# Scores of the backward pass as rows in column strips: extending them to the alternating stretch and the second chain

## The chip, the cores and the metric

The kernel runs on one core of a Trainium2 chip. The time is device microseconds of one execution. A ratio is the mean time of one kernel's fast runs over that of the other's of the same rounds on the same chip, so it is not quite the ratio of the medians quoted beside it. Each ratio comes with its 95% interval.

## The reference, cut to what matters

The program computes one adaLN block in decode (batch 2, one token, 32 heads, a K and V cache of 8192 rows of 128 bf16 per head) and all its gradients. Per head, of which there are 64:

```
scores = K q / sqrt(128);  p = softmax(scores);  o = p V           # forward: reads K and V
x1 = x + ga * (o Wo);  SwiGLU block;  the way back to d_o           # the "chain": short, serial
dp = V d_o                                                          # reads V again
dV = p (outer) d_o;   dK = ds (outer) q,  ds = p * (dp - sum(p*dp)) # writes 2 x 2 MB per head
```

K is read once, V twice (less a few heads kept), dK and dV are written once: 422 MB read and 284 MB written in all. The change concerns `dp = V d_o`, in the code's words "V times dO".

## The kernel before: the parts that matter

The program is laid out by hand in slots (the code below is shortened); a pass over one head takes 8 slots. Passes "A" are forward (K, then V), passes "C" are backward. The first 32 A passes (batch 0) run alone; then the first chain; then, from 500 to 1060 us about, A passes of batch 1 and C passes of batch 0 alternate; then the second chain runs together with 9 C passes; then the rest of the C passes run with the weight gradients.

Every pass transposes its head's blocks on TensorE, eight to a tile `kt`. Scores can then be made in two ways.

```python
def c_s(n, g):
    if n in crow:                                   # as rows, in four strips of 32 columns
        return s_rows(("c", n), n, g, ...)
    for j in range(GRP):                            # as columns: one matmul of one column a block
        nc.tensor.matmul(DP[n][:, cc:cc+1], kt[:, j, :], DO_bf[:, b, h:h+1], ...)

def s_rows(key, i, g, bank):                        # every second group: 4 matmuls of 512 columns
    w = qz[i % NZ][:, NSL-1-a:NSL-1-a+NR]           # weights 128 x 32, one column non-zero
    for j in range(NST):
        nc.tensor.matmul(R_ps[key][NR*j:NR*(j+1), :], w, kt[:, o:o+SW, :], ...)

def rows_out(key): nc.scalar.copy(t, R_ps.pop(key)) # row bank to SBUF (group "srow")
def cols_out(ps, t): ...                            # 4 fp32 matmuls turn it back into columns
```

The outer products of dV and dK are made by VectorE, half a head at a time, and stored from there by a queue that GpSimd issues in order. dK products start 11 slots after the pass's first slot, and one slot later for a head that goes by rows. Below, "M products" are the matmuls of line 480, the A passes' products with V.

```python
halfp = tile_pool(bufs=21)     # 21 tiles of 128 x 8192 bytes: all of K, V, dK, dV pass through them
for q in range(NQ):                                                  # NQ = 4
    at(s + 2*q, PL_TT, lambda: c_dv(n, q))
    at(s + NG + LAG + 1 + (n in crow) + 2*q, PL_DK, lambda: c_dk(n, q))
```

A load waits until one of the 21 half tiles is free. A half tile of dV or dK becomes free after its store.

Of the kernel before, what the change touches and what calls it, by code (L numbers as in the profile page):

```python
# [9 lines left out]
F32 = mybir.dt.float32  # L10
# [7 lines left out]
def kernel(  # L18
# [26 lines left out]
    nc = tc.nc  # L45
    P = 128
# [11 lines left out]
    NHD = B * H  # L58
# [4 lines left out]
    NG = KK // GRP  # L63
# [8 lines left out]
    def hb(i):  # L72
        return i // H, i % H
# [15 lines left out]
    kps = ctx.enter_context(tc.tile_pool(name="kps", bufs=1, space=bass.MemoryType.PSUM))  # L89
# [12 lines left out]
    def mtps():  # L102
        return mps.tile([P, 512], F32, name="m_ps", tag="m_ps")
# [10 lines left out]
    QP = 4  # L114
    NST = 4
    NR = P // NST
# [8 lines left out]
    NSL = KK // (SW * NST)  # L125
# [1 line left out]
    ssel = cst.tile([P, NSL * NST], F32, name="ssel")  # L127
    nc.vector.tensor_copy(ssel[:].rearrange("p (x j) -> p x j", j=NST),
                          identb[:].rearrange("p (j x) -> p x j", j=NST)[:, 0:NSL, :])
    NZ = 3  # L130
    qz = [cst.tile([P, NR + NSL - 1], BF16, name=f"qz{k}") for k in range(NZ)]
    for z in qz:
        nc.vector.memset(z[:], 0.0)
# [4 lines left out]
    def col(name, nch=NC, dt=F32):  # L138
        return cols.tile([P, nch, B], dt, name=name, tag=name)
# [51 lines left out]
    def kb_(store, i, kk):  # L191
        return store[(i, kk // HK)][:, kk % HK, :]

    def vb_(key, kk):
        return V[(key, kk // HK)][:, kk % HK, :]
# [24 lines left out]
    qT_bf = col("qT_bf", H, BF16)  # L220
# [108 lines left out]
    now = [0]  # L329
# [9 lines left out]
    def pump():  # L339
        while loads and free["half"] - keep[0] >= 1:  # L340
            loads.pop(0)[2]()

    def release(n=1):
        free["half"] += n
# [3 lines left out]
    def head_ps():  # L348
        t = stps()
        cur_ps[:] = [t, now[0], 0]  # L350
        return t
# [22 lines left out]
    def transposes(block, dve):  # L374
        tp = tps.tile([P, GRP, P], BF16, name="tp", tag="tp")
        for j in range(GRP):
            nc.tensor.transpose(tp[:, j, :], block(j), identb[:])  # L377
        kt = ktp.tile([P, GRP, P], BF16, name="kt", tag="kt")
        if dve:
            nc.vector.tensor_copy(kt[:], tp[:])  # L380
        else:
            nc.scalar.copy(kt[:], tp[:])  # L382
        return kt
# [3 lines left out]
    def a_t(i, g):  # L387
        b, h = hb(i)
        if g == 0:
            if i in byrows:  # L390
                nc.gpsimd.tensor_copy(qz[i % NZ][:, NSL - 1:NSL], qT_bf[:, h, b:b + 1])
            else:
                S_ps[i] = head_ps()
        kts[(i, g)] = transposes(lambda j: kb_(K, i, g * GRP + j), g in (2, 6))
# [3 lines left out]
    def s_rows(key, i, g, bank):  # L398
        if g % SG < SG - 1:
            return  # L400
        def kt_of(k):
            return (*key, k) if isinstance(key, tuple) else (key, k)
        a = g // SG
        if a == 0:
            R_ps[key] = bank()
        w = qz[i % NZ][:, NSL - 1 - a:NSL - 1 - a + NR]
        for j in range(NST):
            kt = kts[kt_of(g - SG + 1 + j * SW // GRP)]
            o = j * SW % GRP
            nc.tensor.matmul(R_ps[key][NR * j:NR * (j + 1), :], w, kt[:, o:o + SW, :],  # L410
                             start=(a == 0), stop=(a == NSL - 1))
        for k in range(SG):
            kts.pop(kt_of(g - k))
# [18 lines left out]
    def a_s(i, g):  # L432
        if i in byrows:
            return s_rows(i, i, g, mtps)
        b, h = hb(i)
        kt = kts.pop((i, g))
        for j in range(GRP):
            cc = g * GRP + j
            nc.tensor.matmul(S_ps[i][:, cc:cc + 1], kt[:, j, :], qT_bf[:, h, b:b + 1], start=True, stop=True)  # L439
# [106 lines left out]
    def job_a(i, s):  # L546
        x = 1 if i in byrows else 0
        MOFF = moff(i)
        for g in range(NG):
            at(s + g, PL_T, lambda g=g: a_t(i, g))  # L550
            at(s + g + LAG, PL_S, lambda g=g: a_s(i, g))
            at(s + g + MOFF, PL_M, lambda g=g: a_m(i, g))
            at(s + g + MOFF, PL_FREE, lambda g=g: a_free(i, g))
        if x:
            at(s + NG + LAG, PL_EXP, lambda: a_rows(i))
            at(s + NG + LAG + 1, PL_EXP, lambda: a_cols(i))
        at(s + NG + LAG + x, PL_MAX, lambda: a_max(i))
        at(s + NG + LAG + x + 1, PL_MAX, lambda: a_bias(i))
        at(s + NG + LAG + x + 2, PL_EXP, lambda: a_exp(i))
        for q in range(NQ):  # L560
            at(s + NG + LAG + x + 3 + 2 * q, PL_TT, lambda q=q: a_scale(i, q))
        at(s + MOFF, PL_EXP, lambda: a_pz(i))
        at(s + MOFF + 2, PL_T, lambda: a_kp(i))
        at(s + MOFF + 2, PL_FREE, lambda: k_free(i, 0))
        at(s + MOFF + 4, PL_FREE, lambda: k_free(i, 1))
        if i % HPB == HPB - 1:
            at(s + MOFF + 3, PL_EXP, lambda: a_kp_rows(i))
            at(s + MOFF + 4, PL_M, lambda: a_kp_out(i))
        at(s + MOFF + NG - x, PL_EV, lambda: a_evac(i))
# [8 lines left out]
    def end_a(s):  # L578
        return s + MOFF + NG
# [68 lines left out]
    def hcol(name, dt=F32):  # L648
        return cols.tile([P, B, H], dt, name=name, tag=name)
# [7 lines left out]
    DO_bf = hcol("DO_bf", BF16)  # L657
# [384 lines left out]
    def lay(steps, slot):  # L1042
        for n, f in steps:
            at(slot, PL_TASK, f)
            slot += n
        return slot
# [15 lines left out]
    sC = []  # L1062
# [16 lines left out]
    R0 = min([sA[i] for i in byrows], default=sA[NHD - 1])  # L1079
    A_END = end_a(sA[NHD - 1]) + 1  # L1080
# [5 lines left out]
    t1 = lay(ch[1], CS1)  # L1086
# [42 lines left out]
    def c_t(n, g):  # L1129
        if g == 0:  # L1130
            if n in crow:
                b, h = hb(n)
                nc.gpsimd.tensor_copy(qz[n % NZ][:, NSL - 1:NSL], DO_bf[:, b, h:h + 1])
            else:
                DP[n] = head_ps()
        spare = A_END <= now[0] < t1 or now[0] >= max(sC) - 5 * NG
        kts[("c", n, g)] = transposes(lambda j: vb_(("c", n), g * GRP + j), g in (2, 6) and not spare)
        if g % HG == HG - 1:
            V.pop((("c", n), g // HG))
            release()  # L1140
            pump()

    crow = {n for n in range(NHD) if t1 < sC[n] < max(sC) - 4 * NG}

    def c_rows(n):
        kts[("crow", n)] = rows_out(("c", n))
# [4 lines left out]

    def c_s(n, g):
        if n in crow:
            return s_rows(("c", n), n, g, lambda: kps.tile([P, QP * P], F32, name="k_ps", tag="k_ps"))
        b, h = hb(n)
        kt = kts.pop(("c", n, g))
        for j in range(GRP):
            cc = g * GRP + j
            nc.tensor.matmul(DP[n][:, cc:cc + 1], kt[:, j, :], DO_bf[:, b, h:h + 1], start=True, stop=True)  # L1159
# [53 lines left out]
    for n in range(NHD):  # L1213
        s = sC[n]
        for g in range(NG):
            at(s + g, PL_T, lambda n=n, g=g: c_t(n, g))
            at(s + g + LAG, PL_S, lambda n=n, g=g: c_s(n, g))
        at(s - 3, PL_B, lambda n=n: c_spread(n))
        for q in range(NQ):
            at(s + 2 * q, PL_TT, lambda n=n, q=q: c_dv(n, q))  # L1220
            at(s + NG + LAG + 1 + (n in crow) + 2 * q, PL_DK, lambda n=n, q=q: c_dk(n, q))
        x = 1 if n in crow else 0
        if x:
            at(s + NG + LAG, PL_EXP, lambda n=n: c_rows(n))
            at(s + NG + LAG + 1, PL_EXP, lambda n=n: c_cols(n))
        at(s + NG + LAG + x, PL_DS, lambda n=n: c_ds(n))

        for hf in range(2):
            if n not in kept:
                want(s + hf * HG, lambda n=n, hf=hf: load_v(("c", n), n, hf))  # L1230
# [185 lines left out]
    for kc in range(NC):  # L1416
        for half in range(HD // 2048 if HD >= 2048 else 1):
            w = min(2048, HD)
# [27 lines left out]
    for kc in range(NC):  # L1446
        for m0 in range(0, MD, 2048):
            w = min(2048, MD - m0)
# [72 lines left out]
```

## Time and profile before

1744.36 us, median of 6 runs (1740.22 to 1746.57).

The table by stretches of the kernel before. Its columns are: the stretch, its length, busy time (and instructions) of TensorE, its weight loads, VectorE, ScalarE and GpSimd, then the granted TensorE clock, the mean busy share of the 16 DMA engines, and GB/s moved.

```profile
60.00:260.00 200.00, 199.93 (x4125) 185.08 (x4123) 128.41 (x178) 126.86 (x178) 73.69 (x118) 1.00 1.01 416
500.00:1060.00 560.00, 448.61 (x6855) 385.46 (x6853) 387.74 (x457) 296.88 (x444) 84.47 (x243) 0.86 1.01 420
1060.00:1120.00 60.00, 49.06 (x901) 45.88 (x899) 46.88 (x85) 33.07 (x52) 9.36 (x18) 0.75 0.91 358
1120.00:1200.00 80.00, 63.28 (x1317) 59.17 (x1316) 65.56 (x124) 74.32 (x95) 13.32 (x25) 0.93 1.01 412
1200.00:1240.00 40.00, 15.16 (x176) 11.56 (x175) 12.93 (x14) 11.44 (x18) 2.33 (x5) 0.59 1.01 426
1240.00:1600.00 360.00, 282.60 (x2283) 181.43 (x2282) 224.33 (x248) 224.37 (x345) 51.55 (x103) 0.62 1.01 414
```

Of these stretches DMA is saturated in all but 1060 to 1120 us, the start of the second chain. TensorE is called busy for 80% of the alternating stretch, but that is not what limits it. The waits of TensorE in that stretch (engine, line, what it waited for, us in total, times, longest):

```profile
PE tp L377 <- DMA half<-in_A_k_cache_dram: 65.5, 26, 5.7
PE s_ps L430 <- ACT srow L417: 23.1, 22, 1.1
```

and the waits of the queue that issues the loads:

```profile
SPq L187 <- DMA out_dram<-half: 338.9, 64, 11.5
SPq L181 <- DMA out_dram<-half: 102.1, 22, 5.4
```

So TensorE waits for loads of K, and loads wait for stores that free half tiles. The cost of the pieces comes from the timeline of TensorE in that stretch (start, us, engine, line, operation, count). Starts are what to read: durations of pipelined matmuls overlap.

```profile
634.03 0.40 PE L410 MATMUL m_ps<-kt,qz_108 128*32 128x512 bf16 x4
634.37 0.64 PE L480 MATMUL m_ps<-ek,half 128*128 128x129 bf16 x8
...
638.02 1.06 PE L430 MATMUL s_ps<-ssel,srow 128*128 128x16 f32 x8 [1.05 <-ACT srow L417]
638.93 0.94 PE L377 MATMUL tp<-identb,half 128*128 128x128 bf16 x8
639.66 0.40 PE L1159 MATMUL s_ps<-DO_bf,kt 128*128 128x1 bf16 x8
639.92 1.01 PE L377 MATMUL tp<-identb,half 128*128 128x128 bf16 x8
```

Four strip matmuls take 0.34 us from start to next start; eight one-column matmuls take 0.26 us, about 30 ns each; the way back into columns takes 0.91 us after a wait of 1.05 us. The Trainium skill ("TensorEngine Tiling (Array Packing)", section Instruction Overhead) says that a matmul of one column takes as long as one of 60 columns. The lines above agree in kind: eight transposes of 128 columns take 0.73 us (638.93 to 639.66), so 128 times the columns cost 2.8 times the time. A one-column matmul is wasteful by the column but cheap by the piece.

### The profile page before, as it was taken

Reading aid. Unit: us, or ns where it says so; the run is one execution under the profiler, and the core shown is the slowest. Engines: PE = TensorE matmul, PEld = TensorE weight load, DVE = VectorE, ACT = ScalarE, POOL = GpSimd, SP = SyncE. Lnnn points to the kernel's source line nnn. Section 1 sums busy time; section 2 is a strip of 40 time slices with the busy share of each in tenths; the row PEclk is TensorE's granted clock in tenths of the full one; section 3 lists DMA queues with packets and bytes.
Section 4 is the critical chain, followed back from the end, with each engine's and each line's share of the span. In section 5 each row is a group of like instructions: output and inputs, shape, how many; then the busy total and the mean of one; then the engine's idle time right before and its main releaser. Section 6 shows DMA issues by size and latency. Waiting matters only on the chain.

```text
span 1739.6 us, 50825 instructions
## 1 busy us (share of the span) xinstructions
PE 1418.5 (82%) x22083; PEld 1182.0 (68%) x22083; DVE 1154.6 (66%) x1574; ACT 1030.7 (59%) x1506; POOL 328.5 (19%) x696
## 2 busy tenths in 40 slices
PE   6999999989988788778787887885589797775684
PEld 5999998879877676667776666875355454454463
DVE  2666666867876667676676766785566667656676
ACT  4666666646565555455554555696467566665685
POOL 0334333322211111111111111111111111111111
PEclk9999999988988889888888888798655557668787
DMA  9999999999999999999999999999999999999998
GB/s 381 416 416 416 416 416 389 416 383 390 378 397 423 425 424 422 424 408 424 405 423 424 418 411 375 367 422 421 425 404 423 413 416 392 422 417 402 408 418 334
DMA packets 109388, 709.07 MB, mean 408 GB/s; under 512 B 11175, under 2 KB 17683, under 8 KB 27243
## 3 DMA queue, kind: packets, MB, share of 16 engines
q1 hardware_dynamic: 67280, 421.59, 59.7%
q0 software_dynamic: 36864, 268.45, 37.2%
q10 hardware_dynamic: 5019, 15.78, 2.3%
q8 instruction: 173, 2.83, 0.6%
q14 instruction: 52, 0.43, 0.1%
HBM read 421.57 MB, written 284.20 MB: 406 GB/s over the span
## 4 chain that ended last, share of the span: by engine, by line
DMA 33%; PE 33%; issue 21%; DVE 5%; ACT 4%; POOL 3%; SPq 1%; POOLq 0%; ACTq 0%; DVEq 0%
DMA half<-in_A_k_cache_dram 19%; PE tp L377 13%; DMA out_dram<-half 10%; PE m_ps L480 10%; PE s_ps L439 3%; PE k_ps L502 2%; ACT kt L382 2%; POOL out_dram L1187 2%; DVE half L1182 2%; DMA half<-in_A_v_cache_dram 2%; DMA half<-in_w_mod_dram 1%; DVE ek L465 1%; PE m_ps L410 1%; DMA half<-in_A_wo_dram 1%; PE s_ps L430 1%
## 5 line engine op out<-in xcount | busy, mean ns | idle before, releaser
L382 ACT COPY kt<-tp 128x1024 bf16<-128x1024 bf16 x794 | 798.1, 1021 | 600.8 <-PE tp L377 572.3
L377 PE MATMUL tp<-identb,half 128*128 128x128 bf16 x8192 | 734.7, 243 | 114.0 <-DMA half<-in_A_k_cache_dram 69.1
L377 PEld LDWEIGHTS <-half 128*128 128x128 bf16 x8192 | 582.7, 110 | 207.6 <-issue 127.8
L480 PE MATMUL m_ps<-ek,half 128*128 128x129 bf16 x4096 | 341.4, 228 | 4.7 <-DVE ek L465 2.9
L1187 POOL DMA_DIRECT2D out_dram<-half x256 | 136.7, 534 | 985.6 <-DVE half L1182 871.1
L380 DVE COPY kt<-tp 128x1024 bf16<-128x1024 bf16 x230 | 158.4, 689 | 246.3 <-PE tp L377 245.7
L480 PEld LDWEIGHTS <-half 128*128 128x128 bf16 x4096 | 261.5, 101 | 17.1 <-issue 16.7
L1159 PE MATMUL s_ps<-DO_bf,kt 128*128 128x1 bf16 x2496 | 112.7, 166 | 30.0 <-DVE kt L380 15.9
L1159 PEld LDWEIGHTS <-kt 128*128 128x128 bf16 x2496 | 104.6, 102 | 37.0 <-DVE kt L380 16.3
L430 PE MATMUL s_ps<-ssel,srow 128*128 128x16 f32 x400 | 65.0, 297 | 57.5 <-ACT srow L417 57.3
L439 PE MATMUL s_ps<-qT_bf,kt 128*128 128x1 bf16 x2496 | 107.7, 164 | 1.2 <-DVE lnst L1027 0.4
L430 PEld LDWEIGHTS s_ps<-ssel,srow 128*128 128x128 f32 x400 | 60.0, 230 | 67.3 <-ACT srow L417 67.0
L439 PEld LDWEIGHTS <-kt 128*128 128x128 bf16 x2496 | 96.7, 97 | 2.0 <-issue 1.0
L1315 ACT CAST stg<-m_ps 128x512 bf16<-128x512 f32 (+2 forms) x124 | 72.6, 588 | 16.2 <-PE m_ps L1314 7.7
L502 PE MATMUL k_ps<-half,pz 128*32 128x512 bf16 x1024 | 71.7, 402 | 4.6 <-POOL pz L488 4.6
L1314 PE MATMUL m_ps<-half 2*128 2x512 bf16 (+2 forms) x124 | 66.8, 538 | 5.4 <-ACT half L1289 2.8
L451 DVE TENSOR_REDUCE nm<-s_ps 128x1 f32<-128x128 f32 x64 | 18.7, 291 | 52.3 <-PE s_ps L448 52.3
L502 PEld LDWEIGHTS <-pz 128*32 128x32 bf16 x1024 | 22.7, 99 | 27.8 <-POOL pz L488 6.1
L1314 PEld LDWEIGHTS <-half 2*128 2x128 bf16 (+1 forms) x124 | 12.6, 101 | 32.8 <-issue 27.7
L1397 ACT COPY kt<-tp 128x1024 bf16<-128x1024 bf16 x28 | 30.5, 1089 | 4.1 <-PE tp L1391 3.0
L1289 ACT CAST half<-m_ps 2x512 bf16<-2x512 f32 (+1 forms) x36 | 20.2, 565 | 19.0 <-DMA out_dram<-half 14.9
L793 PE MATMUL s_ps<-d_attn_bf,kt 128*128 128x1 bf16 x256 | 11.4, 165 | 22.7 <-DVE kt L780 12.7
(899 smaller groups left out, 1912.5 us busy)
## 6 DMA issues: line engine op xcount, KB each, us to landing
out_dram<-half POOLq DMA_DIRECT2D x256, 1024.0 KB, 13.5
half<-in_A_v_cache_dram SPq DMA_DIRECT2D x252, 1024.0 KB, 16.8
half<-in_A_k_cache_dram SPq DMA_DIRECT2D x128, 1024.0 KB, 19.9
out_dram<-stg ACTq DMA_DIRECT2D x22, 512.0 KB, 9.9
half<-in_A_wq_dram SPq DMA_DIRECT2D x8, 1024.0 KB, 11.6
half<-in_A_wo_dram SPq DMA_DIRECT2D x4, 1024.0 KB, 20.6
half<-in_w_mod_dram SPq DMA_DIRECT2D x3, 1024.0 KB, 16.7
half<-in_B_w_dram SPq DMA_DIRECT2D x3, 1024.0 KB
```

Of the source, the lines that this page charges most:

```text
L377: nc.tensor.transpose(tp[:, j, :], block(j), identb[:])
L380: nc.vector.tensor_copy(kt[:], tp[:])
L382: nc.scalar.copy(kt[:], tp[:])
L430: nc.tensor.matmul(sv[:, c, :], t[:, c * P:(c + 1) * P], ssel[:], start=True, stop=True)
L439: nc.tensor.matmul(S_ps[i][:, cc:cc + 1], kt[:, j, :], qT_bf[:, h, b:b + 1], start=True, stop=True)
L480: nc.tensor.matmul(m[:, 0:P + 1], vb_(i, kk), t[:, kk % QK, 0:P + 1], start=(kk == 0), stop=(kk == KK - 1), skip_group_check=True)
L502: nc.tensor.matmul(kp["ps"][NR * j:NR * (j + 1), :], pz[:, o:o + NR], K[(i, kk // HK)][:, kk % HK:kk % HK + QP, :], start=False, stop=(h = ...
L1159: nc.tensor.matmul(DP[n][:, cc:cc + 1], kt[:, j, :], DO_bf[:, b, h:h + 1], start=True, stop=True)
L1182: nc.vector.tensor_tensor(pair(t[:, o:o + QK, :]), QD[(n, which)][:].rearrange("p (a b) -> p a b", b=2).unsqueeze(1).to_broadcast((P, QK, ...
L1187: sq_.dma_start(src_of(dst, n)[:, hf * HK:(hf + 1) * HK, :], t[:])
L1314: nc.tensor.matmul(ps[:lw, 0:rw], rsl(ln, lc, lw, step), rsl(rn, rc, rw), start=True, stop=True)
L1315: nc.scalar.copy(st["t"][:lw, o:o + rw], ps[:lw, 0:rw])
```

## The change

The intent is to take one-column matmuls from TensorE where passes alternate and in the second chain: 34 more heads take V times dO as rows (before, only 25 late heads did). A fourth weight tile is added so that A and C passes have two each, and the strip rows go to the bank `m_ps` while the bank `k_ps` is in use.

```diff
-    NZ = 3
+    NZ = 4
     qz = [cst.tile([P, NR + NSL - 1], BF16, name=f"qz{k}") for k in range(NZ)]
...
-                nc.gpsimd.tensor_copy(qz[i % NZ][:, NSL - 1:NSL], qT_bf[:, h, b:b + 1])
+                nc.gpsimd.tensor_copy(qz[i % 2][:, NSL - 1:NSL], qT_bf[:, h, b:b + 1])
...
-        w = qz[i % NZ][:, NSL - 1 - a:NSL - 1 - a + NR]
+        w = qz[i % 2 + (2 if isinstance(key, tuple) else 0)][:, NSL - 1 - a:NSL - 1 - a + NR]
...
-                nc.gpsimd.tensor_copy(qz[n % NZ][:, NSL - 1:NSL], DO_bf[:, b, h:h + 1])
+                nc.gpsimd.tensor_copy(qz[2 + n % 2][:, NSL - 1:NSL], DO_bf[:, b, h:h + 1])
...
-    crow = {n for n in range(NHD) if t1 < sC[n] < max(sC) - 4 * NG}
+    crow = {n for n in range(NHD) if R0 < sC[n] < max(sC) - 4 * NG}
+
+    def c_bank():
+        if now[0] <= A_END:
+            return mtps()
+        return kps.tile([P, QP * P], F32, name="k_ps", tag="k_ps")
...
-            return s_rows(("c", n), n, g, lambda: kps.tile([P, QP * P], F32, name="k_ps", tag="k_ps"))
+            return s_rows(("c", n), n, g, c_bank)
```

`R0` is the first slot of the alternating stretch, `A_END` the end of the last A pass, `t1` the end of the second chain, with the products with its weight that make d_o. One side effect is not in the diff: `(n in crow)` in the slots of dK is now 1 for 34 more heads.

## The prediction

> **What bounds the kernel now.** The table by stage (busy time of each engine in stretches) has a DMA share of about 1.0 nearly everywhere: 416 GB/s in the first passes, 420 at 500 to 1060 us, where passes alternate, 415 at 1200 to 1600. 709 MB at 420 GB/s are 1688 us of the 1740. The Trainium skill ("DMA: Bandwidth & Descriptors", section Bandwidth) gives a fabric ceiling of 435 GB/s and a measured 425 for large transfers; the best stretches here, 423 to 427, agree. So TensorE savings can shorten the alternating stretch by 1% at most. There TensorE waits 65.5 us for loads of K, and the load queue waits 441 us for stores that free buffers. DMA is short of work only at 1060 to 1120 us (share 0.91, 358 GB/s) (the second chain begins) and at the tail.
>
> **What the change does.** By count of the slots, 34 more heads take V times dO as rows: 25 in the alternating stretch, 9 in the second chain. A head loses 64 one-column matmuls; each group of 8 advances TensorE by 0.20 to 0.26 us, so 1.6 to 2.1 us. It gains 4 groups of 4 strip matmuls (0.33 us each, 1.3 us), 4 fp32 matmuls that bring the row back into columns (0.9 us), a copy of 0.60 us on ScalarE, and a wait of TensorE for that copy (1.05 us where rows are used now). For TensorE that is even, or +1 us a head with the wait. dK products start one slot later, transposed tiles are held up to a slot longer in a ring of 4, and V's strip rows share the M bank.
>
> **How much is on the critical path.** While passes alternate, a period of 25 us holds nearly 3 us of TensorE waiting for K, so +1 us a head disappears there. In the second chain ScalarE is saturated (74 of 80 us at 1120 to 1200), and 8 or 9 copies add 5 us; the ring of transposed tiles, shared with the chain's own, may add 5 us of stalls. But at 1200 to 1240 TensorE and ScalarE are both under 40% busy, and the chain of waits has 32.6 us of stores there. So compute runs ahead of DMA, and a delay of 5 to 10 us is mostly eaten by that wait, unless DMA runs dry meanwhile.
>
> **Prediction: 1746 us, 1735 to 1760 in 8 of 10.** Faster by over 2%: 0.02; within 2%: 0.95; slower by over 2%: 0.03.
>
> **What would show it.** (1) Alternating stretch: GB/s within 1%, length within 5 us. (2) One-column matmuls of dO fall from 2496 to 320, row copies on ScalarE rise from 50 to 84, still 0.60 us each. (3) TensorE's wait for that copy rises by 1 us a head, its wait for K falls. (4) The second chain is 0 to 10 us longer, ScalarE over 90% busy, the DMA wait after it shorter by as much. (5) The span is within 10 us.
>
> **What would make it wrong.** DMA runs dry in the second chain because the ring couples ScalarE to TensorE more tightly: slower by 10 to 30 us. Or the bank shared with M makes alternating passes wait on each other, so that loads start later. Or TensorE, not buffers, set the gap at 1060 to 1120: then up to 9 us (60 us times 1 - 358/420) come back, and it is faster by 0.5%.

## More of the kernel before

Last, the stores of the second chain as GpSimd issues them (start, us, engine, line, operation, then the idle time before it and what ended it):

```profile
1107.97 0.53 POOL L1187 DMA_DIRECT2D out_dram<-half  x1 [6.85 <-DVE half L1182]
1111.13 0.53 POOL L1187 DMA_DIRECT2D out_dram<-half  x1 [2.63 <-DVE half L1182]
1119.06 0.53 POOL L1187 DMA_DIRECT2D out_dram<-half  x1 [7.40 <-DVE prod L800]
1120.40 0.53 POOL L1187 DMA_DIRECT2D out_dram<-half  x1 [0.81 <-DVE ds_22661 L1203]
1127.67 0.53 POOL L1187 DMA_DIRECT2D out_dram<-half  x1 [6.74 <-DVE dacc L1003]
1128.88 0.53 POOL L1187 DMA_DIRECT2D out_dram<-half  x1 [0.67 <-DVE half L1182]
```

## The result, and the profile after

1742.55 us median (1740.52 to 1745.41, 10 runs) against 1744.19 us: ratio 0.999, interval 0.9981 to 1.000. The same.

The stretches of the changed kernel, with the same columns:

```profile
60.00:260.00 200.00, 200.00 (x4136) 185.09 (x4134) 128.75 (x180) 127.06 (x178) 74.38 (x119) 1.00 1.01 418
500.00:1060.00 560.00, 454.88 (x5971) 356.51 (x5969) 383.72 (x458) 309.33 (x472) 97.33 (x264) 0.91 1.01 420
1060.00:1120.00 60.00, 50.83 (x744) 42.34 (x743) 43.90 (x84) 32.63 (x48) 11.09 (x23) 0.72 0.87 325
1120.00:1200.00 80.00, 65.11 (x994) 52.96 (x991) 61.17 (x113) 73.00 (x97) 14.43 (x28) 0.91 0.99 402
1200.00:1240.00 40.00, 18.79 (x172) 13.38 (x169) 15.96 (x20) 12.80 (x20) 3.54 (x7) 0.60 1.01 426
1240.00:1600.00 360.00, 291.54 (x2276) 186.10 (x2276) 224.13 (x247) 224.90 (x345) 52.89 (x103) 0.59 1.01 414
```

The alternating stretch has 884 TensorE instructions less and the same 420 GB/s. The second chain moves less: 325 and 402 GB/s against 358 and 412. And the first line has 418 GB/s where it had 416, in a stretch whose program the change doesn't touch. The waits of TensorE in the alternating stretch:

```profile
PE tp L377 <- DMA half<-in_A_k_cache_dram: 55.3, 26, 4.4
PE s_ps L430 <- ACT srow L417: 27.1, 22, 1.2
```

and of the load queue:

```profile
SPq L187 <- DMA out_dram<-half: 302.8, 45, 14.4
SPq L181 <- DMA out_dram<-half: 186.9, 43, 5.4
```

The added work was taken out of the wait for K (65.5 to 55.3 us); the loads wait for stores as before (490 us against 441). The stores of the second chain:

```profile
1106.09 0.53 POOL L1192 DMA_DIRECT2D out_dram<-half  x1 [11.64 <-DVE half L1187]
1107.22 0.53 POOL L1192 DMA_DIRECT2D out_dram<-half  x1 [0.60 <-DVE half L1187]
...
1116.08 0.53 POOL L1192 DMA_DIRECT2D out_dram<-half  x1 [8.12 <-DVE half L1187]
1117.21 0.53 POOL L1192 DMA_DIRECT2D out_dram<-half  x1 [0.60 <-DVE SIG L806]
1127.78 0.53 POOL L1192 DMA_DIRECT2D out_dram<-half  x1 [10.04 <-DVE half L1187]
1128.92 0.53 POOL L1192 DMA_DIRECT2D out_dram<-half  x1 [0.60 <-DVE dacc L1003]
```

They now come in pairs 1.1 us apart, with gaps of 8 to 12 us between pairs. Before, some came close together too (1119.06 and 1120.40, 1127.67 and 1128.88), but the gaps were 7.4 us at most. The change has put dK products one slot later, from odd slots into even ones, the slots in which VectorE makes the next pass's dV products.

**A ledger of bytes.** Since DMA is the limit, I compare the kernels by the bytes they have moved by a given time: the sum of GB/s times 10 us over the windows of 10 us of each profile. The table is relative to a second profile of the kernel before; 1 MB is worth 2.4 us at 420 GB/s. It is my own sum from the profiles, and fixed times cover slightly different work in kernels that are ahead by some us.

```
MB moved more than the second profile of the kernel before, by the time (us)
kernel                  320    560    1060   1200   1600  | gained 560-1060, 1060-1200
before, first profile  +0.06  -0.11  +0.10  +0.36  +0.86  |  +0.21   +0.26
before_pair            -0.02  +0.83  +0.82  -1.96  -1.31  |  -0.01   -2.78
before_a128            +0.60  +1.31  +2.19  +1.25  +1.81  |  +0.88   -0.94
before_a0              +2.57  +4.19  +4.20  +5.62  +4.42  |  +0.01   +1.42
chain_only             +0.61  +1.89  +1.77  -1.76  -1.52  |  -0.12   -3.53
after                  +0.70  +2.53  +3.08  +0.56  +1.35  |  +0.55   -2.52
after_again            +0.63  +1.61  +2.07  -1.82  -1.44  |  +0.46   -3.89
alt_only               +0.61  +1.84  +1.90  +2.75  +2.57  |  +0.06   +0.85
dk_odd                 +0.61  +2.13  +2.54  +2.15  +3.10  |  +0.41   -0.39
alt_odd                +0.75  +1.93  +2.37  +4.00  +4.58  |  +0.44   +1.63
alt_odd_a0             +1.76  +4.76  +4.55  +7.47  +8.30  |  -0.21   +2.92
```

For the changed kernel, something is gained before 560 us and lost again in the second chain, and the alternating stretch, which the change was made for, does nothing. The experiments take these three apart. Two profiles of one kernel can differ by 0.9 MB in a stretch, and by 1.4 in the second chain, for no reason that I know (the two of the kernel before by 0.3; the changed kernel's two by 0.9 before 560 us and by 1.4 in the second chain), so only larger differences, or those that all profiles of a kind share, count.

### The profile page after: what moved, and what is told of

It is laid out like the page before. It is cut to its first block, busy times and chain, and to the rows that moved or that the text cites. A ratio compares the mean times of both kernels' runs of the same rounds, so it can differ in the third digit from the quotient of the medians.

```text
span 1740.2 us, 48279 instructions
## 1 busy us (share of the span) xinstructions
PE 1455.7 (84%) x20723; PEld 1155.3 (66%) x20723; DVE 1150.5 (66%) x1575; ACT 1048.1 (60%) x1540; POOL 348.9 (20%) x730
## 4 chain that ended last, share of the span: by engine, by line
DMA 30%; PE 29%; issue 29%; DVE 5%; POOL 4%; ACT 2%; SPq 1%; POOLq 0%; DVEq 0%; ACTq 0%
DMA half<-in_A_k_cache_dram 15%; DMA out_dram<-half 12%; PE tp L377 12%; PE m_ps L480 8%; POOL out_dram L1192 3%; DVE half L1187 2%; PE s_ps L439 2%; PE k_ps L502 2%; PE m_ps L410 2%; PE s_ps L430 1%; DVE ek L465 1%; ACT kt L382 1%; DMA half<-in_w_mod_dram 1%; DMA half<-in_A_wo_dram 1%; POOL qz_109 L1133 0%
## 5 line engine op out<-in xcount | busy, mean ns | idle before, releaser
L480 PE MATMUL m_ps<-ek,half 128*128 128x129 bf16 x4096 | 334.0, 225 | 5.4 <-DVE OK L544 2.7
L430 PE MATMUL s_ps<-ssel,srow 128*128 128x16 f32 x672 | 105.9, 292 | 45.7 <-ACT srow L417 45.3
L430 PEld LDWEIGHTS s_ps<-ssel,srow 128*128 128x128 f32 x672 | 98.9, 226 | 58.4 <-ACT srow L417 57.7
L439 PEld LDWEIGHTS <-kt 128*128 128x128 bf16 x2496 | 96.8, 97 | 1.2 <-issue 1.0
L1319 PE MATMUL m_ps<-half 2*128 2x512 bf16 (+2 forms) x124 | 70.9, 572 | 3.0 <-ACT half L1294 3.0
L502 PE MATMUL k_ps<-half,pz 128*32 128x512 bf16 x1024 | 67.9, 386 | 2.4 <-POOL pz L488 2.4
L410 PE MATMUL k_ps<-kt,qz_109 128*32 128x512 bf16 x272 | 38.4, 554 | 0.0
L410 PE MATMUL k_ps<-kt,qz_110 128*32 128x512 bf16 x256 | 33.7, 517 | 0.0
L417 ACT COPY srow<-m_ps 128x512 f32<-128x512 f32 x51 | 30.5, 599 | 0.0
```

The lines of the kernel that those rows point to most:

```text
L410: nc.tensor.matmul(R_ps[key][NR * j:NR * (j + 1), :], w, kt[:, o:o + SW, :], start=(a == 0), stop=(a == NSL - 1))
L430: nc.tensor.matmul(sv[:, c, :], t[:, c * P:(c + 1) * P], ssel[:], start=True, stop=True)
L439: nc.tensor.matmul(S_ps[i][:, cc:cc + 1], kt[:, j, :], qT_bf[:, h, b:b + 1], start=True, stop=True)
L480: nc.tensor.matmul(m[:, 0:P + 1], vb_(i, kk), t[:, kk % QK, 0:P + 1], start=(kk == 0), stop=(kk == KK - 1), skip_group_check=True)
L502: nc.tensor.matmul(kp["ps"][NR * j:NR * (j + 1), :], pz[:, o:o + NR], K[(i, kk // HK)][:, kk % HK:kk % HK + QP, :], start=False, stop=(h = ...
L1319: nc.tensor.matmul(ps[:lw, 0:rw], rsl(ln, lc, lw, step), rsl(rn, rc, rw), start=True, stop=True)
```

## The experiments

My theory: while passes alternate, rows change nothing since DMA is the limit; the second chain loses bytes. The rival: rows gain time while passes alternate, and the second chain loses as much. In the second chain, the loss could come from the pairing of products, or else from the added copies and the ring of four transposed tiles.

### 1. The change again, and its two halves

`after_again` is the changed kernel. `alt_only` has rows in the alternating stretch alone (25 heads added), `chain_only` in the second chain alone (9 heads added):

```diff
 # alt_only
-    crow = {n for n in range(NHD) if R0 < sC[n] < max(sC) - 4 * NG}
+    crow = {n for n in range(NHD) if R0 < sC[n] < max(sC) - 4 * NG
+            and not sA[NHD - 1] + NG < sC[n] < t1}
 # chain_only
+    crow = {n for n in range(NHD) if sA[NHD - 1] + NG < sC[n] < max(sC) - 4 * NG}
```

> The changed kernel once more, beside its parts on the same chip. Theory (bound by DMA; the strips change nothing on the critical path while passes alternate, and what the second chain loses is mostly eaten by the wait for DMA after it): 0.997 to 1.001 of the kernel before. Rival (TensorE time was removed and came back in full): below 0.995.

> Rows for V times dO only while passes alternate (25 heads), columns in the second chain. Theory: 0.997 to 1.001 of before, the stretch from 1060 to 1140 us has its DMA share back at that of before (mean about 0.93 or more), and the stretch from the last M product to the last product of the second chain's weight is back to about 100 us (99.7 before, 109.7 changed). Rival (gain in the alternating stretch and an equal loss in the second chain cancel): below 0.996, 7 us or more.

> Rows only in the second chain (9 heads), columns while passes alternate. Theory: the second chain takes 105 to 112 us as in the changed kernel, the time is 0.999 to 1.004 of before because the DMA wait after the chain eats most of it. Rival (gain and loss cancel): above 1.004.

Measured, over 1745.41 us of the kernel before in the same rounds: `after_again` 1744.48 us, 0.9992 (0.9976 to 1.0008); `alt_only` 1736.22 us, 0.9949 (0.9934 to 0.9964); `chain_only` 1747.44 us, 1.0014 (0.9998 to 1.0029).

So the rival seemed right: there is a gain of 0.5% without the second chain's rows, and they cost 1744.48 - 1736.22 = 8 us. But the ledger puts no part of the gain into the alternating stretch: `alt_only` gains 0.06 MB there. It is already ahead by 0.61 MB at 320 us, where the rows have not begun. That was new, and experiment 4 follows it up.

### 2. Is it the pairing?

`dk_odd` is the changed kernel with the dK products of row heads one slot later still, so in odd slots again. `before_pair` does the reverse in the kernel before: it keeps columns, adds no strip and no copy, and only moves the dK products of the 9 heads of the second chain into even slots.

```diff
 # dk_odd
-    at(s + NG + LAG + 1 + (n in crow) + 2 * q, PL_DK, ...)
+    at(s + NG + LAG + 1 + 2 * (n in crow) + 2 * q, PL_DK, ...)
 # before_pair
+    at(s + NG + LAG + 1 + (n in crow or sA[NHD - 1] + NG < s < t1) + 2 * q, PL_DK, ...)
```

> The changed kernel with the dK products of row heads one slot later still, so that they no longer fall in the same slots as the next pass's dV products (in the changed kernel the stores of the second chain come in pairs 1.1 us apart with gaps of 8 to 12 us; before, they were spread). Theory that this pairing makes the second chain run dry of DMA: stores single again there, DMA share at 1060 to 1140 us up from 0.90 to 0.93 or more, second chain 100 to 105 us. Rival (the ring of 4 transposed tiles or the chain of copies does it): second chain stays at 107 us or more. Total time 0.995 to 1.001 in either case.

> The kernel before with columns everywhere it had them; only the dK products of the 9 heads of the second chain start one slot later, so that they share slots with the next pass's dV products, as rows make them do in the changed kernel. No strip products and no copies are added. Theory (pairing of the two products of VectorE starves the stores): the stretch 1060 to 1140 us moves 2 to 3.5 MB less than in the kernel that has rows only while passes alternate, and the time is 1.002 to 1.005 of before. Rival (strips, copies or the ring of tiles cost it): 0.999 to 1.001, bytes as before.

Measured: `dk_odd` 1738.67 us, 0.9960 (0.9942 to 0.9978), over 1745.41; `before_pair` 1749.61 us, 1.0027 (1.0014 to 1.0040), over 1744.29. The stores of `before_pair`:

```profile
1102.24 0.53 POOL L1187 DMA_DIRECT2D out_dram<-half  x1 [1.70 <-DVE half L1182]
1113.05 0.53 POOL L1187 DMA_DIRECT2D out_dram<-half  x1 [10.28 <-DVE half L1182]
1114.18 0.53 POOL L1187 DMA_DIRECT2D out_dram<-half  x1 [0.60 <-DVE half L1182]
1123.08 0.53 POOL L1187 DMA_DIRECT2D out_dram<-half  x1 [8.37 <-DVE ds L1203]
```

and of `dk_odd`:

```profile
1104.90 0.53 POOL L1192 DMA_DIRECT2D out_dram<-half  x1 [8.30 <-DVE half L1187]
1106.77 0.53 POOL L1192 DMA_DIRECT2D out_dram<-half  x1 [1.34 <-PE k_ps L410]
...
1114.62 0.53 POOL L1192 DMA_DIRECT2D out_dram<-half  x1 [7.13 <-DVE half L1187]
1118.19 0.53 POOL L1192 DMA_DIRECT2D out_dram<-half  x1 [3.03 <-DVE dacc L1003]
1124.02 0.53 POOL L1192 DMA_DIRECT2D out_dram<-half  x1 [5.30 <-DVE half L1187]
```

The pairing alone, without any rows, loses 2.78 MB in the second chain, inside the 2.5 to 3.9 MB of the kernels with rows there. Taking it away from the rows brings the loss to 0.39 MB. In all four profiles with paired products that stretch loses 2.5 MB or more, and in none of the seven others more than 0.94. So the pairing is the cause of the lost bytes. That dK comes later is not: `dk_odd` has it later still. What remains for copies, strips and the ring of transposed tiles in the second chain is within the spread of the profiles. In time, the pairing costs 5 to 6 us (1749.61 - 1744.29; 1744.48 - 1738.67) of the 8 us above. (I meant to enlarge the ring as well; neither 5 nor 6 tiles fit into SBUF, so that was not tried.)

`dk_odd` expected a second chain of 100 to 105 us, from the last M product to the last product that makes d_o. It took 1192.5 - 1086.0 = 106.5 us against 109.7, so by that measure it missed; the DMA share at 1060 to 1140 us, 0.93, and the time were as expected. By the same measure `before_pair` took 1201.8 - 1096.8 = 105.0 us and `alt_only` 1189.0 - 1087.9 = 101.1 us, against 99.7 before. So the pairing explains only about half of the 10 us by which the chain grew. The rest comes with the rows, whether by copies, strips or the ring, and with the stores spread (`dk_odd`) it costs no bytes and no time that these runs resolve. That is one profile each.

### 3. What are rows worth where DMA does not bind?

`before_nodv` and `after_nodv` leave out the dV stores of the 25 heads of the alternating stretch (that output is not fully written). Their outputs are wrong, which doesn't matter for the times.

```diff
-            sq_.dma_start(src_of(dst, n)[:, hf * HK:(hf + 1) * HK, :], t[:])
+            if not (which == 1 and sC[n] <= sA[NHD - 1] + NG):
+                sq_.dma_start(src_of(dst, n)[:, hf * HK:(hf + 1) * HK, :], t[:])
```

> Wrong on purpose: the kernel before without the dV stores of the 25 heads of the alternating stretch, 52 MB less to move (105 MB of dV and dK stores there fall to 52). Theory, bound by DMA: at 420 GB/s up to 125 us are gained until the engines bind; I expect 60 to 120 us, DMA share in that stretch below 0.97, and K waits of TensorE nearly gone. Rival, TensorE and its waits bind the stretch already: under 20 us.

> Wrong on purpose: the changed kernel without the same dV stores. It tells what rows are worth where DMA has spare room. By my costs (TensorE about even, or 1 us a head more with the wait for the copy) it is 0 to 25 us slower than the kernel before without these stores. Rival, rows do save TensorE time that DMA hides: over 10 us faster than it.

Measured, over 1744.29 us: `before_nodv` 1644.07 us, 0.9432 (0.9414 to 0.9449); `after_nodv` 1657.05 us, 0.9496 (0.9480 to 0.9513). 52 MB less gave 100 us (at 420 GB/s they are 125 us), so DMA, or the half tiles that its stores hold, was the limit, and not TensorE. The wait for K at 500 to 1060 us fell from 65.5 us to this in `before_nodv`:

```profile
PE tp L377 <- DMA half<-in_A_k_cache_dram: 3.7, 2, 2.1
```

The DMA share at 500 to 900 us was 0.98 and not below 0.97 as I expected, so DMA still was close behind. With this room, the change makes the kernel 13 us slower. From the first product that makes d_o to the last M product (the end of the A passes) `before_nodv` took 996.3 - 452.2 = 544.1 us and `after_nodv` 1001.1 - 450.6 = 550.5 us: 6.4 us over 25 heads, about 0.26 us a head. That is one profile each, and two profiles of the changed kernel differ by 3.8 us in this measure (638.3 and 642.1 us, below). The second chain, where the products are paired, took 97.8 against 111.7 us, 13.9 us more. Some 7 us of these 20 came back elsewhere; the placement of experiment 4 may explain about 5, but was not measured in these kernels. Rows in strips saved instructions here, and no TensorE time that shows.

### 4. Where do the first 320 us gain 0.6 MB?

The fourth `qz` tile takes 96 bytes per partition, and all tiles allocated after it move by that. Read from the built programs, the 21 half tiles start 32 bytes past a multiple of 256 before, and 128 past one after. `before_again` checks that the first profile of the kernel before was no accident. `before_a128` adds 96 unused bytes to the kernel before. `before_a0` moves the half tiles alone, to a multiple of 256.

```diff
 # before_a128
+    cst.tile([P, 48], BF16, name="pad")
     for z in qz:
 # before_a0: the half tiles first, behind one tile of 128 bytes that exists anyway
+    selp = ctx.enter_context(tc.tile_pool(name="selp", bufs=1))
+    halfp = ctx.enter_context(tc.tile_pool(name="halfp", bufs=NHALF))
     cst = ctx.enter_context(tc.tile_pool(name="cst", bufs=1))
...
-    halfp = ctx.enter_context(tc.tile_pool(name="halfp", bufs=NHALF))
...
-    sel = cst.tile([P, NR], F32, name="sel")
+    sel = selp.tile([P, NR], F32, name="sel")
```

> The kernel before, once more, for a second profile of it. The first profile of it has moved 1 to 2.7 MB less by 520 us than every profile of the variants, although the programs are the same until about 455 us; if that is chance of one execution, this profile lies among the variants there (1.0 to 2.7 MB more than the first profile by 520 us) and its span is 1738 to 1748 us. If it is of the kernel, it repeats the first profile within 0.5 MB.

> The kernel before with 96 unused bytes per partition ahead of its tiles, nothing else. The change's fourth strip-weight tile moved every large SBUF tile by the same 96 bytes, from 32 to 128 past a multiple of 256 (read from the built programs), and every profile of a kernel with that tile shows 418 GB/s at 60 to 260 us against 416 in the three profiles without it, 0.34 MB more by 160 us and 0.6 MB by 320 us. Theory, the placement does that: 418 GB/s there, 0.5 to 0.7 MB more by 320 us, time 0.995 to 0.999 of before (1.5 us from the first passes alone, up to 7 us if the whole run profits). Rival, it comes from the instruction stream: 416 GB/s and 0.999 to 1.001.

> The kernel before with only the large tiles (the half heads that loads fill and stores empty) moved, to a multiple of 256; all small tiles stay at 32 past one. Theory, it is the placement of the DMA's tiles that counts and a multiple of 256 is at least as good as 128 past it: 418 to 421 GB/s at 60 to 260 us, 0.993 to 0.999 of before. Rival, the small tiles that the engines read count: 416 GB/s and 1.000.

Measured: `before_again` 1744.51 us, 1.0001 (0.9981 to 1.0022); its bytes repeat the first profile's within 0.11 MB at 320, 560 and 1060 us. `before_a128` 1740.26 us, 0.9965 (0.9951 to 0.9979), and `before_a0` 1730.86 us, 0.9917 (0.9903 to 0.9930), over 1745.49 us; `before_a0` gained more than expected. The first passes, of `before_a128` and then of `before_a0`:

```profile
60.00:260.00 200.00, 200.00 (x4137) 185.09 (x4135) 128.69 (x179) 126.96 (x178) 74.20 (x119) 1.00 1.01 418
520.00:900.00 380.00, 302.60 (x4662) 260.58 (x4660) 264.34 (x313) 202.39 (x303) 55.77 (x165) 0.86 1.01 421
```

```profile
60.00:260.00 200.00, 200.00 (x4140) 185.11 (x4138) 128.82 (x180) 127.59 (x179) 73.62 (x116) 1.00 1.01 424
520.00:900.00 380.00, 304.20 (x4685) 261.75 (x4685) 264.25 (x313) 203.86 (x307) 57.02 (x165) 0.86 1.01 422
```

The same program moves 416, 418 or 424 GB/s there depending on where its half tiles start, and the DMA share reads 1.01 each time. `before_a128` takes over the whole advantage of the changed kernel at 320 us (0.60 MB against 0.61 to 0.75). Where loads and stores mix the rates are 420, 421 and 422: placement counts above all where only loads run. The lead at 320 us is worth 1.4 and 6.1 us of the 5 and 15 us gained (0.60 and 2.57 MB at 420 GB/s); where the rest is won is not resolved. Relative to 256, `before_a0` moves only the half tiles and five small tables of constants, so the tiles that DMA fills are most likely what counts; `alt_odd_a0` below has its other small tiles 96 bytes further on and moves 424 GB/s here too. But the edit also puts the half tiles some 16 KB lower in SBUF (from 32800 to 16640 in the built programs), and no run separates that from the multiple of 256.

The Trainium skill ("DMA: Bandwidth & Descriptors", section How a descriptor splits into AXI transactions) says that a transaction must start at a multiple of 256 bytes, so that a descriptor starting elsewhere costs extra beats of 32 bytes. That the tiles at a multiple of 256 did best, 424 GB/s, fits it. By an estimate from its rule, 32 past costs one extra beat and 128 past four; the runs have it the other way round (416 and 418 GB/s). But the page tells the rule for bytes that are read, and loads write the half tiles, so it may not bear on them. So the times are shown, and the mechanism is open.

### 5. A version that uses what was found

`alt_odd` has the rows of `alt_only` and the dK slots of `dk_odd`. `alt_odd_a0` also has the half tiles at a multiple of 256, by the same edit as in `before_a0`.

> Candidate: rows while passes alternate and after the chain, columns in the second chain, and dK products of row heads in the odd slots, apart from the dV products. It adds up what rows only while passes alternate (0.9949) and dK in odd slots (0.9960) gave, as far as these are different stretches: bytes by 1200 us as with rows only while passes alternate (2.75 MB over the second profile of before), and 0.5 to 1.3 MB more gained after 1240 us. Expected 0.991 to 0.995. If both gains are the same one, 0.995.

> The same candidate with the large tiles at a multiple of 256 as well. If placement beyond the first passes matters, 1 to 5 us faster than the candidate; if 128 past a multiple is as good, equal within 2 us.

Measured, over 1745.49 us: `alt_odd` 1734.79 us, 0.9936 (0.9922 to 0.9949); `alt_odd_a0` 1722.31 us, 0.9872 (0.9859 to 0.9886). Both give right results. `alt_odd_a0` is 23 us faster than the kernel before and about 20 us faster than the changed one; the step from 128 past a multiple to the multiple (with the 16 KB) is worth 12.5 us of it, more than I expected. Whether `alt_odd` beats `alt_only` is not clear: their intervals overlap, and they ran in different rounds.

## Why the prediction was right or wrong

The time was right: 1746 us forecast, 1742.55 measured, "within 2%" at 0.95. It was right partly by luck: two terms that I did not have cancelled in part.

- "TensorE savings can shorten the alternating stretch by 1% at most": nothing speaks against it, but the change did not test it, for it saved no TensorE time (448.61 us busy before, 454.88 after). The stretch moved 420 GB/s before and after, all kernels lie within 1.1 MB of each other there, with rows or without, and without dV stores time fell by 100 us.
- "For TensorE that is even, or +1 us a head with the wait": it fits. The stretch without dV stores shows +0.26 us a head, little beyond the spread. My sign (3), the wait for the copy to rise by 1 us a head, failed: it rose from 23.1 to 27.1 us, 0.16 us a head. 44 copies caused 22 waits, so half of them were hidden. I took the wait of the A passes for that of any pass.
- Sign (2), 320 one-column matmuls of dO and 84 copies at 0.60 us: right (320; 51 of 599 ns and 33 more).
- Sign (1), the alternating stretch alike in rate and length: right. From the first product that makes d_o to the last M product it took 641.1 us before, and 638.3 and 642.1 us after.
- Sign (4), "the second chain is 0 to 10 us longer": it took 109.7 and 109.9 us against 99.7, at the edge. ScalarE stayed over 90% busy (73.0 of 80 us). The idle time after it did get shorter: TensorE idled 21.2 of 40 us at 1200 to 1240 against 24.8. Yet no bytes came back. Sign (5) held (spans 1739.6 and 1740.2 us).
- The step that failed: "a delay of 5 to 10 us is mostly eaten by that wait". The ledger of the changed kernels is level from 1200 to 1600 us (+0.56 to +1.35, -1.82 to -1.44). TensorE's wait for DMA after the chain is the sign of a DMA that is already at its maximum, so bytes that were not moved in the second chain cannot be caught up. Such a wait takes up a delay of compute only if DMA stays fed during that delay. I had named the exception ("unless DMA runs dry meanwhile") and given it no weight. The rows of the second chain cost 8 us of time (`alt_only` against `after_again`), 5 to 6 of them by the pairing.
- The cause of the lost bytes was wrong too: I blamed the ring of transposed tiles and the copies. The pairing of dK and dV products does it. Where the stores stayed spread (`dk_odd`, chain 106.5 us), a delay of 5 us was eaten, as far as these runs resolve it. I had written "dK products start one slot later" and looked no further than at how long a buffer is held.
- The term that I missed: the placement of the half tiles, worth 1745.49 - 1740.26 = 5 us. It offset part of the second chain's loss.

The sum, in medians of different rounds: about -5 us by placement, +8 us by the rows of the second chain, mostly their paired products, and the rest, -4 us or so, not resolved: `alt_only` is 0.16% faster than `before_a128` by ratios of two different rounds, with intervals of 0.15% each.

## What to carry to other kernels

In a kernel whose DMA is at its limit nearly everywhere, ask of each change what it does to the stretches where DMA is not, and in which order and at what spacing stores are issued there: bytes lost in a dry stretch were not won back here, and an idle engine afterwards did not absorb them. Compare two profiles by the bytes moved so far; it shows in which stretch time was won or lost even when the totals are equal. And when a change adds or drops a small tile, compare a stretch that it doesn't touch: if that became faster or slower, the placement of the other tiles may have changed with it, and is worth tuning by itself.

## What the Trainium skill lacked or had wrong

- "DMA: Bandwidth & Descriptors", section How a descriptor splits into AXI transactions: it gives beats but no rate for loads of 8 KB rows into SBUF tiles that start off a multiple of 256 bytes. Here: 416 GB/s at 32 past, 418 at 128 past, 424 at a multiple, and 5 and 15 us of 1745. Its count of beats, told for reads, would put 128 past behind 32 past. (The tiles at a multiple also lie 16 KB lower.)
- "SBUF — State Buffer", section Operand start alignment, says of DMA that it is right at any element-aligned address, and that its runs timed nothing. The numbers above are such times for three placements.
- No page says that bytes lost where DMA runs dry are not won back where it is saturated. Here 2.8 MB lost by paired stores in `before_pair`, with no other change, made it 0.27% slower.
